# An mLSTM cell and a gated product on one core: gates of four chunks in one call, and half passes for the second chunk's first product

## The chip, the cores and the metric

One Trainium2 chip, one of its cores. The kernel is one program with its instructions in the order in which the source issues them, one stream for each engine: PE (TensorE), DVE (VectorE), ACT (ScalarE), POOL (GpSimd) and SP (SyncE, which here only issues DMAs). ACT and POOL issue some DMAs too. The metric is the device time of one execution in microseconds (us). The time of a kernel is the median over its runs.

## The reference, cut to what matters

Eight inputs and one output, all float32. B = 4 batches, H = 8 heads, S = 768 steps, head dimension D = 40; the second part takes 3072 rows (b, s) of 320 values.

```
for t in range(S):                                  # for each b, h
    m_new  = max(f[t] + m, i[t])
    C = exp(f[t] + m - m_new) * C + exp(i[t] - m_new) * outer(v[t], k[t])
    n = exp(f[t] + m - m_new) * n + exp(i[t] - m_new) * k[t]
    m = m_new
    y[t] = sigmoid(o[t]) * (C @ q[t]) / max(|n . q[t]|, 1)
x = y as (B*S, H*D) = (3072, 320)
h = x @ w_in                                        # 320 -> 2048
out = (h * sigmoid(1.702 * h)) @ w_out              # 2048 -> 320
```

The maximum m runs through time; within a chunk of steps it is a running sum of f and a running maximum (a scan), and from one chunk to the next only one value for each (b, h) is carried.

## The kernel before, in words

**Chunks.** Time is cut into six chunks w = 0 to 5 of L = 128 steps. A chunk has three stages: attention (the recurrence as a masked product within the chunk, plus a carried state), the first product, called "up" (512 rows of x by w_in), and the second product, "down" (by w_out). The attention of chunk w+1 is laid between the blocks of the down stage of chunk w (function `attention` gives the order, `run(side.get(i, []))` at line 1342 issues it after block i). Chunk 0 has an up of its own in full float32 (`up`), and its down (`down`) has 16 blocks. Later chunks' downs (`down_fast`, from line 1023) have 14 blocks.

**The order of the work** is written by hand (`manual_schedule`): each engine runs its instructions in source order, and an instruction that waits holds up all that is behind it on its engine or queue. Data dependences become semaphore waits. Buffers come from pools that turn round by tag; a tile waits until the last user of its buffer has finished.

**Gates.** `gates(w)` (line 302) works on 32 partitions, one for each (b, h), with 128 steps beside each other: two scans, the maximum at the half and at the end of the chunk, the differences that the weights need, and a swap of the two halves of 64 steps for the odd heads (by the factors `odd` and `even`, which `masks()` makes). `gates_out(w)` (343) stores the results to DRAM in five DMAs (`m_row`, `st_row`, `d_row`), `columns_in(w)` (371) loads them back with time on the partitions (`raw`, five DMAs) and `spread(w)` (423) loads `m_row`, broadcast to 64 partitions, into the two `wt` tiles (four DMAs, L430). `columns_turn`, `columns` and `weights_exp` (466) turn these into the weights. `side_queue(w)` sends the DMAs of chunk 1 by POOL's queue and the others by SP's. The call for chunk 1 stands at j = 3 of chunk 0's up, that of chunk 2 at j = 0 of chunk 1's up, those of chunks 3 to 5 at block 7 of the down two chunks before. `load_gates(w)` issues two loads for each chunk.

**The up stage of chunk 1 and later.** A float32 product is built of several passes of type fp32r: x and w_in are each split into a part rounded by the factor BIAS (`x_high`, `w_high`) and the rest in two forms (`x_low`, `x_diff`, `w_low`, `w_diff`); results come from two sums in PSUM, `side` and `main`. The 16 blocks of 128 columns go in eight pairs j = 0 to 7. The 320 features of x are two groups of 128 and a last one of 64. For chunk 1, `up_fast` (848) does 16 passes of 128x128 by 512 for each pair, 128 in all, the last 64 features in full passes too (`x_rest`, `w_rest`). For chunks 2 to 5, `up_strips` (923) does the last 64 features in passes that use 64 of the 128 rows of the array, and it does the terms `low`, `high`, `diff` as such half passes for every pair from the second on: `halves` issues two that lie on different halves of the rows and run at the same time. They need one more weight, `w_strip` (for chunk 2 on made by `strip_weights`, 777, in chunk 1's down), and one more split of x (the last lines of `split_on`, line 835).

**Notes.** Of two sets of half passes that add to the same bank, the second may start only when the first has finished. `seen` (917) puts an empty instruction on ACT's queue which waits for the first set; the first pass of the second set waits for that note (`behind`, 912).

```
    def seen(w, mm):
        note = (A if w + 1 < NW else nc.sync).nop()
        tc.add_manual_dep(note.ins, mm.ins.name, SYNC)
```

**Around each pair:** `evict_side` (963, ACT) scales `side` into g; `evict_main` (968, DVE, L971) adds `main`; `gelu_fast` (840, ACT) applies the gelu in place; POOL makes differences and sums for the down stage.

**The splits of w_in** are made once, in four quarters n of 256 rows by 512 columns: `split_high` (740, ACT), `split_diff` (743, DVE L745), `split_low` (748, DVE L751). Quarters 0 and 1 before chunk 1's up, 2 and 3 within it. `keep` (753) stores `w_diff` of each quarter and `w_low` of quarters 2 and 3 to DRAM from ACT's queue (L755), and later chunks fetch them. `keep_last` (757) copies `w_low` of quarter 3 into another tile on ACT, and SP stores that at j = 5.

**Counting.** `count` adds up to `COUNTS[w]` semaphore increments to PE's stream, one behind a pass; nothing waits for them.

The loop over j of chunks 1 to 4 (lines 1231 to 1296) issues `up_fast` or `up_strips`, then whatever of the splits, stores, fills and transposes for the next chunk belongs to that j:

```
for j in range(NF // 2):
    (up_strips if by_strips(w) else up_fast)(w, j)
    ...
        if j == 2:
            split_high(3)
            keep(w_diff_row, 2, w_diff[1, 2])
            keep(w_low_row, 2, w_low[1, 2])
            split_diff(3)
            split_low(3, V)
```

Of the kernel before, what the change touches and what calls it, by code (L numbers as in the profile page):

```python
# [8 lines left out]
FP = mybir.dt.float32  # L9
# [16 lines left out]
COUNTS = {0: 54, 1: 128, 2: 105, 3: 105}  # L26
# [9 lines left out]
def kernel(  # L36
# [178 lines left out]
    one1 = const.tile([BH, 1], FP, name="one1")  # L215
# [3 lines left out]
    ones = one1.to_broadcast([BH, L])  # L219
# [9 lines left out]
    odd, even = (const.tile([3 * BH, 1], FP, name=n) for n in ("odd", "even"))  # L229
# [10 lines left out]
    cols, stacked, m_row, raw = {}, {}, {}, {}  # L240
# [61 lines left out]
    def gates(w):  # L302
# [30 lines left out]
        if w:  # L333
            for x in range(2):
                V.tensor_scalar(out=swapped[:, x * HL:(x + 1) * HL], in0=st[:, (1 - x) * HL:(2 - x) * HL], scalar1=odd,
                                scalar2=None, op0=OP.mult)
            V.scalar_tensor_tensor(out=swapped, in0=st, scalar=even, in1=swapped, op0=OP.mult, op1=OP.add)
            both = ends[w] = gate.tile([BH, 2], FP, name="both")
            V.tensor_tensor(out=both[:, 0:1], in0=m, in1=mid, op=OP.subtract)
            V.tensor_tensor(out=both[:, 1:2], in0=mid, in1=end, op=OP.subtract)  # L340
            stacked[w] = m_run, swapped, both

    def gates_out(w):
        m_run, swapped, both = stacked[w]
        to = m_row[w] = rows.tile([2, BH, HL], FP, name="m_row")
        side_queue(w).dma_start(out=to[:, 0::2].rearrange("n h t -> h n t"),
                          in_=m_run[0::2].rearrange("h (n t) -> h n t", t=HL))
        for n in range(2):
            side_queue(w).dma_start(out=to[1 - n, 1::2], in_=m_run[1::2, n * HL:(n + 1) * HL])
        st_row = rows.tile([L // 32, 3 * BH, 32], FP, name="st_row")  # L350
        d_row = rows.tile([BH, 2], FP, name="d_row")
        stacked[w] = st_row, d_row
        side_queue(w).dma_start(out=st_row.rearrange("n k t -> k n t"), in_=swapped.rearrange("k (n t) -> k n t", t=32))
        side_queue(w).dma_start(out=d_row, in_=both)
# [11 lines left out]
    def masks():  # L366
        V.tensor_reduce(out=odd, in_=full.rearrange("p (j two) -> p two j", two=2)[:, 1], axis=AX.X, op=OP.add)
        V.memset(odd[BH:2 * BH, :], 0.0)
        V.tensor_scalar(out=even, in0=odd, scalar1=-1.0, scalar2=1.0, op0=OP.mult, op1=OP.add)

    def columns_in(w):
# [3 lines left out]
        for n in range(L // 32):  # L375
            side_queue(w).dma_start(out=x[n * 32:n * 32 + 32, 0:3 * BH].rearrange("r (k t) -> r k t", t=32),
                              in_=st_row[n].rearrange("(k r) t -> r k t", r=BH))
# [46 lines left out]
    def spread(w):  # L424

        for c in range(2):
# [281 lines left out]
    w_high, w_low, w_diff, w_rest = {}, {}, {}, []  # L708
# [11 lines left out]
    def by_strips(w):  # L720
        return w > 1

    def rooms(w):
# [4 lines left out]
        if w > 1:  # L728
            w_low.update({(w, n): gp.tile([128, 2, 512], FR, tag="g", name="w_low")
                          for n in ((2, 3) if by_strips(w) else (2,))})  # L730
# [4 lines left out]
    def more_rooms(w):  # L735

        w_low[w, 3], w_diff[w, 2], w_low[w, 2], w_diff[w, 3] = (gp.tile([128, 2, 512], FR, tag="g", name=name)
                                                                for name in ("w_low", "w_diff", "w_low", "w_diff"))
# [18 lines left out]
    def keep_last():  # L757
        w_low[3] = work.tile([128, 2, 512], FR, tag="wx", bufs=1, name="w_low")
        A.copy(out=w_low[3], in_=w_low.pop((1, 3)))

# [15 lines left out]

    def strip_weights():

        wr = w_rest[0]
        w_rest.append(work.tile([128, NF // 2, 128], FR, tag="wx", bufs=1, name="w_strip"))  # L780
        d, low, high = w_rest[1], wr[64:128], wr[0:64]
# [12 lines left out]
    def split_x(w, c):  # L794
# [9 lines left out]
        A.activation(out=x_rest[w][0][:, t], in_=x[:, 2], func=AF.Copy, scale=BIAS if by_strips(w) else -BIAS / BASE)  # L804
# [9 lines left out]
    def split_x_rest(w, c):  # L814
        t, x = part_of(w, c)
        both, other = x_rest[w]
        if by_strips(w):
            V.scalar_tensor_tensor(out=other[:, t], in0=both[:, t], scalar=-1.0 - 1.0 / BASE, in1=x[:, 2], op0=OP.mult,
                                   op1=OP.add)
        else:  # L820
            V.scalar_tensor_tensor(out=other[:, t], in0=x[:, 2], scalar=-1.0 / BASE, in1=both[:, t], op0=OP.mult,
                                   op1=OP.subtract)
# [6 lines left out]
    def split_on(w):  # L829
# [5 lines left out]
        if by_strips(w):  # L835
            both, other = x_rest[w]
            V.scalar_tensor_tensor(out=both[64:128], in0=other[64:128], scalar=BASE, in1=both[64:128], op0=OP.mult,
                                   op1=OP.add)
# [8 lines left out]

    def up_fast(w, j):

        n = j // 2  # L850
        col = lambda i: slice((2 * j + i) % 4 * 128, (2 * j + i) % 4 * 128 + 128)
        low = w_low.get((w, n), w_low.get(n))
        if j % 2:
            side, main = ([bank() for _ in range(2)] for _ in range(2))
        else:
            side, main = ([both[:, i, :] for i in range(2)] for both in (banks("p_h"), banks("p_h")))
        parts = [(main, k, lambda i, k=k: w_high[n][:, k, col(i)], x_high[w][:, k]) for k in range(2)]
        parts += [(main, 2 + k, lambda i, k=k: low[:, k, col(i)], x_low[w][:, k]) for k in range(2)]
        parts += [(side, k, lambda i: w_rest[0][:, 2 * j + i], x) for k, x in enumerate(x_rest[w])]
        parts += [(side, 2 + k, lambda i, k=k: w_diff[w, n][:, k, col(i)], x_diff[w][k]) for k in range(2)]  # L860

        def passes(which, i, first=False, last=False):
            for m in which:
# [555 lines left out]
```

## Time and profile before

| | us |
|---|---|
| median of three runs | 438.42 |
| the runs | 437.18, 438.42, 440.49 |
| the profiled execution: its time | 438.98 |
| its span in the trace | 437.3 |

The stages in the trace, each from its first pass to that of the next (microseconds from the start of the span):

| from | to | length | what runs on PE |
|---|---|---|---|
| 0.00 | 108.15 | 108.15 | all stages of chunk 0, attention of chunk 1 |
| 108.15 | 137.79 | 29.64 | up of chunk 1 |
| 137.79 | 176.63 | 38.84 | down of chunk 1, attention of chunk 2 |
| 176.63 | 204.71 | 28.08 | up of chunk 2 |
| 204.71 | 243.47 | 38.76 | down of chunk 2, attention of chunk 3 |
| 243.47 | 271.72 | 28.25 | up of chunk 3 |
| 271.72 | 437.30 | 165.58 | the rest |

How to read the lines below. A line of the windows gives start, end and length of a stretch, then busy time and number of instructions of PE, PEld (weight loads), DVE, ACT and POOL, then the granted TensorE clock (1.00 is full speed), the busy share of the DMA engines and GB/s. A line of the timeline gives start and duration, engine, source line, operation, the tiles out<-in with their shapes, and in brackets how long the engine stood idle before it and what ended that. "q" behind an engine's name is its queue of instructions that are not counted as busy, such as DMA issues. A line of DMA issues gives the number of issues, KB each and the median us from issue to landing.

### The profile page before, as it was taken

The numbers are of one execution on the slowest core, as the hardware profiler recorded it, in microseconds if no ns is written. First come the engines' busy times: TensorE is split into PE (matmuls) and PEld (weight loads), VectorE is DVE, ScalarE is ACT, GpSimd is POOL, SyncE is SP. The second block draws the span as 40 slices with busy tenths as digits, with TensorE's granted clock in tenths as the row PEclk, the third lists the DMA queues.
The fourth block names the chain that finished last, engine by engine and source line by source line (L and its number), as shares of the span: only waits on it lengthen the run. The fifth ranks groups of instructions, "written<-read, shape, count | busy, mean of one in ns | idle before, by whom it ended". The sixth has DMA issues, their size and how long they took to land.

```text
span 437.3 us, 13451 instructions
## 1 busy us (share of the span) xinstructions
PE 431.9 (99%) x5342; PEld 375.0 (86%) x5342; DVE 353.5 (81%) x689; ACT 247.2 (57%) x540; POOL 146.7 (34%) x155
## 2 busy tenths in 40 slices
PE   8999999999999999999999999999999999999996
PEld 6877887777888999888999888999887999888996
DVE  4898998989889799659789659789759759779990
ACT  5677779922777900397900386900287940298720
POOL 6411326533056822035712035622036624013100
PEclk9999999999999999999999999999999999999999
DMA  8999999217797516999306997605998925820000
GB/s 169 188 285 193 254 252 225 66 34 186 198 206 152 127 49 156 312 161 172 54 31 146 311 178 154 86 19 131 282 197 151 121 66 125 258 98 2 0 32 30
DMA packets 130733, 64.07 MB, mean 147 GB/s; under 512 B 102208, under 2 KB 122672, under 8 KB 130672
## 3 DMA queue, kind: packets, MB, share of 16 engines
q1 hardware_dynamic: 121232, 57.48, 59.4%
q10 hardware_dynamic: 8768, 4.28, 3.4%
q0 software_dynamic: 672, 1.46, 1.2%
q8 instruction: 43, 0.70, 0.7%
q14 instruction: 18, 0.15, 0.1%
HBM read 51.86 MB, written 11.34 MB: 145 GB/s over the span
## 4 chain that ended last, share of the span: by engine, by line
PE 94%; ACT 2%; DVE 1%; DMA 1%; issue 0%; SPq 0%; DVEq 0%
PE p_out L1036 26%; PE p_h L911 13%; PE p L911 10%; PE p_out L979 8%; PE p_h L663 7%; PE p L1114 5%; PE p L865 3%; PE p_h L865 3%; PE p L931 3%; PE p L540 2%; PE p L548 2%; PE p L496 2%; PE p_h L673 2%; PE p_out L1114 2%; PE p L639 2%; PE p L412 1%
## 5 line engine op out<-in xcount | busy, mean ns | idle before, releaser
L803 ACT ACTIVATE x_high<-xT 128x512 fp32r<-128x512 f32 x10 | 6.3, 631 | 88.4 <-DVE xT L609 88.4
L1036 PE MATMUL p_out<-w_out,g 128*128 128x160 f32 x384 | 55.5, 301 | 0.0
L1036 PEld LDWEIGHTS p_out<-w_out,g 128*128 128x128 f32 x384 | 52.9, 190 | 1.6 <-ACT g L966 1.3
L843 ACT ACTIVATE g<-g 128x512 f32<-128x512 f32 x80 | 45.7, 629 | 1.9 <-DVE g L971 1.6
L1004 POOL TENSOR_TENSOR g<-g 128x512 f32<-128x512 f32 x16 | 20.5, 1302 | 69.9 <-ACT g L843 63.1
L971 DVE SCALAR_TENSOR_TENSOR g<-p,g 128x512 f32<-128x512 f32 x40 | 25.7, 684 | 22.5 <-PE p L911 19.2
L966 ACT ACTIVATE g<-p 128x512 f32<-128x512 f32 x40 | 21.7, 596 | 34.9 <-PE p L911 29.8
L469 ACT ACTIVATE wt<-wt,cols 128x64 f32<-128x64 f32 x160 | 38.9, 335 | 0.1
L1036 PE MATMUL p_out<-t_sb,s 128*128 128x160 f32 x256 | 37.8, 301 | 0.0
L1036 PEld LDWEIGHTS p_out<-t_sb,s 128*128 128x128 f32 x256 | 35.5, 190 | 0.2
L979 PE MATMUL p_out<-w_out,g 128*128 128x320 f32 x128 | 35.7, 436 | 0.0
L971 DVE SCALAR_TENSOR_TENSOR g<-p_h,g 128x512 f32<-128x512 f32 x40 | 25.7, 687 | 11.9 <-PE p_h L911 11.9
L979 PEld LDWEIGHTS p_out<-w_out,g 128*128 128x128 f32 x128 | 24.0, 190 | 9.5
L1021 POOL TENSOR_TENSOR s<-g,s 128x256 f32<-128x256 f32 x16 | 12.9, 835 | 52.8 <-PE p_out L1036 52.8
L663 PE MATMUL p_h<-xT,w_in 128*128 128x256 f32 x128 | 29.8, 385 | 0.1
L663 PEld LDWEIGHTS p_h<-xT,w_in 128*128 128x128 f32 x128 | 23.6, 190 | 5.4 <-issue 2.2
L966 ACT ACTIVATE g<-p_h 128x512 f32<-128x512 f32 x40 | 21.6, 593 | 10.3 <-PE p_h L911 9.2
L476 POOL TENSOR_SCALAR_AFFINE_SELECT wt<-wt 64x1024 f32<-64x1024 f32 x20 | 24.3, 1214 | 6.9 <-ACT wt L469 6.0
L625 POOL TENSOR_TENSOR vw<-v_st,cols 128x656 f32<-128x656 f32 (+1 forms) x13 | 16.7, 1301 | 25.0 <-PE p_out L1036 15.4
L1041 DVE TENSOR_TENSOR o_sb<-o_sb,p_out 128x160 f32<-128x160 f32 x56 | 16.3, 314 | 9.7 <-PE p_out L1036 9.2
L421 DVE STREAM_TRANSPOSE qT<-q_sq 128x512 f32<-128x512 f32 x20 | 20.4, 1109 | 1.2 <-ACT q_sq L122 1.2
L911 PE MATMUL p_h<-x_diff,w_diff 64*128 64x512 f32 x128 | 20.3, 395 | 0.0
(260 smaller groups left out, 1097.2 us busy)
## 6 DMA issues: line engine op xcount, KB each, us to landing
w_diff<-w_row SPq DMA_DIRECT2D x16, 512.0 KB, 4.8
wt<-m_row SPq DMA_DIRECT2D x20, 256.0 KB, 5.3
bits<-in_moe_w_in_dram SPq DMA_DIRECT2D x8, 512.0 KB, 9.5
w_low<-w_row SPq DMA_DIRECT2D x8, 512.0 KB, 6.2
out_dram<-o_sb SPq DMA_DIRECT2D x24, 160.0 KB, 2.9
q_sq<-in_q_dram SPq DMA_DIRECT2D x10, 320.0 KB, 8.1
eo<-in_o_gate_dram SPq DMA_DIRECT2D x5, 640.0 KB, 7.4
bits<-in_moe_w_out_dram SPq DMA_DIRECT2D x8, 320.0 KB, 5.4
```

The lines of the kernel that those rows point to most:

```text
L469: A.activation(out=x[:, h, :], in_=x[:, h, :], func=AF.Exp, scale=-1.0, bias=cols[w][:, c * PH + h:c * PH + h + 1])
L476: G.affine_select(out=r, in_=r, compare_op=OP.is_ge, fill=0.0, base=0, pattern=[[0, PH], [1, HL]], channel_multiplier=-1)
L663: T.matmul(ph[j][i][:, t], w_in[f // 4][:, c, f % 4 * 128:f % 4 * 128 + 128], x[:, c, t], start=(first and c == 0 and n == 0), stop=(not f ...
L843: A.activation(out=g, in_=g, func=AF.Gelu_apprx_sigmoid)
L865: T.matmul(dst[i], a(i), x, start=(first and m == which[0]), stop=(last and m == which[-1]))
L911: mm = T.matmul(to[f], a(f)[r], x[r], start=(first and n == 0), stop=(last and n + 1 == len(parts)))
L966: A.activation(out=g[:, i, :], in_=opened[w, j][0][i], func=AF.Copy, scale=-BASE)
L971: V.scalar_tensor_tensor(out=g[:, i, :], in0=opened[w, j][1][i], scalar=1.0 + 1.0 / BASE, in1=g[:, i, :], op0=OP.mult, op1=OP.add)
L979: T.matmul(po, gs[w, f // 2][:, f % 2, b * L:(b + 1) * L], w_out_sb[f // NH][:, f % NH, :], start=(f == 0), stop=(f == NF - 1))
L1004: G.tensor_tensor(out=a10, in0=a00, in1=a10, op=OP.subtract)
L1036: T.matmul(po, a(f), b[:, f, :], start=(f == 0), stop=(f == NH - 1))
L1114: T.matmul((main, side, main)[n], g_part[n, b, f // 2][:, f % 2], wo[n, f][0][:, wo[n, f][1]], start=(f == order[0] and n < 2), stop=(f == ...
```

## The change

It has these parts.

1. **Chunk 1's up by half passes.** `up_fast` is gone and `up_strips` serves chunk 1 too. The weight it needs, `w_strip[1]`, is made by a new `first_strip` (one DVE operation of 128x1024, at block 9 of chunk 0's down, from `rest_high` and `rest_low`). `split_x` and `split_x_rest` lose their second form, and the extra DVE split at the end of `split_on` is done for chunk 1 as well. Chunk 1's increments start at pair 0 instead of pair 1 and number 154; `down_fast` has a `count(1)` behind each pass for those that are left over.
2. **The order in chunk 1's up.** The splits of quarter 3 move from j = 2 to j = 3 (`split_high(3)` stays at j = 2 but behind a fill), both of its stores go out by ACT's queue at j = 3, and `keep_last` with SP's store goes; so `w_low` of quarter 3 stays in its first tile, now of pool `sp`. The fill of `q_sq` moves from j = 3 to j = 2, the transposes that follow it from j = 3 to j = 2, and the second half of the broadcast of `m_row` from j = 2 to j = 7. Gelus come in the order of a table `late`.
3. **Gates of chunks 1 to 4 at once.** `load_four` loads the gates of four chunks into 128 partitions (eight loads on SP's queue, ahead of chunk 1's k), `gates_four` runs once in place of `gates(1)`, and `four_out` stores the results of some chunks: chunk 1's on POOL's queue in the old place, those of chunks 2 to 4 together by SP at block 3 of chunk 0's down. `gates` stays for chunks 0 and 5.
4. **Masks:** `odd` and `even` have 128 rows; ahead of `gates(5)` 32 of them are set back by two memsets.

```diff
-COUNTS = {0: 54, 1: 128, 2: 105, 3: 105}
+COUNTS = {0: 54, 1: 154, 2: 105, 3: 105}
...
+    def load_four():
+        x = work.tile([L, 768], FP, tag="y", name="gates4")
+        four["in"] = [x[:, n * L:(n + 1) * L] for n in range(4)]
+        for n, src in enumerate((f_gate, i_gate)):
+            for x in range(4):
+                nc.sync.dma_start(out=four["in"][n][x * BH:(x + 1) * BH],
+                                  in_=src[:, :, (x + 1) * L:(x + 2) * L].rearrange("b h s -> (b h) s"))
+
+    def gates_four():
...
+        V.tensor_tensor_scan(out=f_run, data0=ones4, data1=f, initial=0.0, op0=OP.mult, op1=OP.add)
+        V.tensor_tensor(out=a, in0=i, in1=f_run, op=OP.subtract)
+        V.tensor_tensor_scan(out=m_run, data0=ones4, data1=a, initial=NEG, op0=OP.mult, op1=OP.max)
+        V.tensor_copy(out=m[0:BH], in_=m_at[1])
+        for n in range(4):
+            r = slice(n * BH, (n + 1) * BH)
+            V.scalar_tensor_tensor(out=m[(n + 1) * BH:(n + 2) * BH] if n < 3 else m_at[NW - 1], in0=m_run[r, L - 1:L],
+                                   scalar=m[r], in1=f_run[r, L - 1:L], op0=OP.max, op1=OP.add)
+        V.tensor_scalar(out=m_run, in0=m_run, scalar1=m, scalar2=None, op0=OP.max)
...
+    def four_out(queue, w0, w1):
+        m_run, swapped, both = (x[(w0 - 1) * BH:(w1 - 1) * BH] for x in four["out"])
...
+        store_max(queue, to, m_run)
+        queue.dma_start(out=st_row.rearrange("k n h t -> h (k n) t"),
+                        in_=swapped.rearrange("h k (n t) -> h (k n) t", t=32))
+        queue.dma_start(out=d_row, in_=both)
...
-    def spread(w):
+    def spread(w, cs=range(2)):
...
-        w_low[w, 3], w_diff[w, 2], w_low[w, 2], w_diff[w, 3] = (gp.tile([128, 2, 512], FR, tag="g", name=name)
-                                                                for name in ("w_low", "w_diff", "w_low", "w_diff"))
+        w_low[w, 3] = sp.tile([128, 2, 512], FR, tag="g", name="w_low")
+        w_diff[w, 2], w_low[w, 2], w_diff[w, 3] = (gp.tile([128, 2, 512], FR, tag="g", name=name)
+                                                   for name in ("w_diff", "w_low", "w_diff"))
...
-    def keep_last():
-        w_low[3] = work.tile([128, 2, 512], FR, tag="wx", bufs=1, name="w_low")
-        A.copy(out=w_low[3], in_=w_low.pop((1, 3)))
...
+    def first_strip():
+        w_strip[1] = work.tile([128, NF // 2, 128], FR, tag="wt", bufs=2, name="w_strip")
+        V.scalar_tensor_tensor(out=w_strip[1], in0=rest_high, scalar=-1.0 / BASE, in1=rest_low, op0=OP.mult, op1=OP.add)
...
-    def up_fast(w, j):
...
-        late = j < 3 and w + 1 < NW
-        for n in ((), (), (0, 1))[j] if late else (j - 1,) if w + 1 < NW or j + 1 < NF // 2 else ():
+        late = {1: (), 2: (), 3: (0, 1), 4: (2,), 5: (3, 4)} if w == 1 else {1: (), 2: (0, 1)} if w + 1 < NW else {7: ()}
+        for n in late.get(j, (j - 1,)):
             gelu_fast(w, n)
...
-    load_gates(1)
-    load(1, "k")
...
     seam(0, 0, 1)
+    load_four()
+    load(1, "k")
...
                 if j == 3:
                     masks()
-                    gates(1)
-                    gates_out(1)
+                    gates_four()
+                    four_out(G, 1, 2)
                     columns_in(1)
...
-                (up_strips if by_strips(w) else up_fast)(w, j)
+                up_strips(w, j)
...
                     if j == 2:
-                        split_high(3)
                         keep(w_diff_row, 2, w_diff[1, 2])
                         keep(w_low_row, 2, w_low[1, 2])
+                    if j == 3:
                         split_diff(3)
                         split_low(3, V)
-                        sums_from = w_low[1, 3].bitcast(FP)[:, 0, :]
-                    if j == 3:
                         keep(w_diff_row, 3, w_diff[1, 3])
-                        keep_last()
-                        wait_for(sums_from)
+                        wait_for(w_low[1, 3].bitcast(FP)[:, 0, :])
                         weight_sums(2)
-                    if j == 5:
-                        keep(w_low_row, 3, w_low[3], nc.sync)
-                if more and j in (1, 3):
-                    fill_squares(q_sq if j == 3 else k_sq)
+                        keep(w_low_row, 3, w_low[1, 3])
+                if more and j in (1, 2 if w == 1 else 3):
+                    fill_squares(k_sq if j == 1 else q_sq)
+                if w == 1 and j == 2:
+                    split_high(3)
...
-                    spread(w + 1)
+                    spread(w + 1, range(1 if w == 1 else 2))
                     load(w + 1, "k")
-                if more and j:
-                    for n in ((), (), (0, 2), (4, 6), (1, 3), (5, 7), ())[j - 1]:
+                if w == 1 and j == 7:
+                    spread(2, (1,))
+                if more:
+                    for n in {2 if w == 1 else 3: (0, 2), 4: (4, 6), 5: (1, 3), 6: (5, 7)}.get(j, ()):
                         block_transposes(w + 1, n)
...
+            if w == 0 and i == 3:
+                four_out(nc.sync, 2, NW - 1)
...
                 split_diff(0)
                 split_low(0, V)
+                first_strip()
```

## The prediction

> **What bounds the kernel now.** I read the page's busy times first, then the chain of work that ended last, then the stages one by one. Times of day are microseconds from the start of the span.
>
> ```profile
> PE 431.9 (99%) x5342; PEld 375.0 (86%) x5342; DVE 353.5 (81%) x689; ACT 247.2 (57%) x540; POOL 146.7 (34%) x155
> PEclk9999999999999999999999999999999999999999
> PE 94%; ACT 2%; DVE 1%; DMA 1%; issue 0%; SPq 0%; DVEq 0%
> ```
>
> TensorE is in flight for 431.9 of 437.3 and 94% of the chain is its own passes. So a microsecond is won only by a pass that goes away, and lost only where PE must wait. The granted clock is at its top digit in all slices.
>
> The stretches between the first pass of an "up" stage and the first `p_out` pass after it, for chunk 1 (to be changed) and chunk 2 (already by half passes), with busy times in the order PE, PEld, DVE, ACT, POOL:
>
> ```profile
> 108.15:137.79 29.64, 29.64 (x130) 24.22 (x129) 26.30 (x43) 22.47 (x39) 12.49 (x10) 1.00 0.78 191
> 176.63:204.71 28.08, 28.08 (x231) 22.40 (x230) 19.30 (x29) 18.36 (x33) 10.05 (x8) 1.00 0.99 210
> ```
>
> Both stages are PE without a gap. Chunk 1 has 128 full passes; chunk 2 does the product in 120 pass times and is 1.56 shorter. But DVE is busy for 26.3 of 29.6 in chunk 1 and for 19.3 of 28.1 in chunk 2: chunk 1 also splits the weights. The timeline gives the places that matter, two engines of chunk 1 and then chunk 2:
>
> ```profile
> 112.90 1.29 DVE L971 SCALAR_TENSOR_TENSOR g<-p,g 128x512 f32<-128x512 f32 x2 [1.24 <-ACT g L966]
> 117.44 1.27 DVE L971 SCALAR_TENSOR_TENSOR g<-p_h,g 128x512 f32<-128x512 f32 x2
> 118.64 1.20 DVE L745 SCALAR_TENSOR_TENSOR w_diff<-w_high,w_in 128x1024 fp32r<-128x1024 f32 x1
> 119.77 1.21 DVE L751 TENSOR_TENSOR w_low<-w_in,w_high 128x1024 fp32r<-128x1024 f32 x1
> ...
> 114.23 0.84 ACTq L755 DMA_DIRECT2D w_row<-w_diff  x2
> 121.46 0.45 ACTq L755 DMA_DIRECT2D w_row<-w_low  x1
> ...
> 176.63 1.20 PE L931 MATMUL p<-x_high,w_high 128*128 128x512 f32 x4
> 191.44 0.63 PE L911 MATMUL p<-x_low,w_low 64*128 64x512 f32 x4
> 193.73 0.63 PE L911 MATMUL p<-x_low,w_low 64*128 64x512 f32 x4
> ...
> 191.71 1.29 DVE L971 SCALAR_TENSOR_TENSOR g<-p_h,g 128x512 f32<-128x512 f32 x2 [2.16 <-PE p_h L911]
> ```
>
> To be seen: the store at 114.23 needs only `w_diff` tiles finished by 111, yet starts 0.04 after the eviction of 112.90 to 114.19, for which the gelu ahead of it on ACT's queue waits. ACT's queue stands still at an unmet wait and everything behind it stands too. And in chunk 2 the fourth pair's main eviction starts 15.08 after the first pass, and the fifth pair's second set of half passes 17.10 after it.
>
> **The change part by part.** *Half passes for chunk 1.* Removed: 128 passes; added: 120 pass times (12 full, 216 half passes that run in twos). Chunk 2 gives 28.08 for this, chunk 3 28.25 by its own first passes (243.47 to 271.72), so the gain is 1.56 or 1.39. I take 1.56.
>
> *The wait that comes with it.* Each second set of half passes waits for a note: an empty ACT instruction that itself waits for the first set (line 919). The old form had no notes. A note stands in ACT's queue behind whatever the program put there before it. The change puts the stores of the last weight quarter (its `w_diff` and `w_low`, from DVE's lines 745 and 751) behind pair 3 and so ahead of pair 4's note. With chunk 1's first pass at 108.15, pair 3's main eviction can start at 108.15 + 15.08 = 123.23. DVE gets there in time: pair 1's eviction at 116.34 (by 184.82 - 176.63), two splits until 119.89, pair 2's eviction until 121.0, two transposes of 2.02 until 123.0. Then by the spacing of the rows above: 1.20 for the eviction, 1.13 for the first split, 1.22 for the second: `w_low` is ready at 126.78. ACT then issues the store, 0.45, and passes the note at 127.2. PE wants to begin its second set at 108.15 + 17.10 = 125.25. Stall: about 1.95 if the issue holds the note back, 1.53 if not; no less than that unless the eviction comes before its product. The upper end, if pair 2's work is a microsecond late, is 3. I take 1.9. Behind the note stand pair 4's side eviction and three gelus, which then run late by as much; they feed evictions and the second product, both after 138.
>
> The trace has no PE gap of this length to show what it does to the clock: from 5 to 430 it shows granted 1.00 and no wait longer than some tenths. [...]
>
> *The end of the stage.* PE leaves it at 137.79 - 1.56 + 1.9 = 138.1. DVE's last transposes then end at 138.6 and the last eviction starts there (138.74 before); ACT's gelus, table load and exponentials (142.73 before) keep their places. The old stall of 0.22 at 151.4, where `p_s` waits for DVE's L648, stays. Nothing is added.
>
> *Splits before the stage.* DVE gets `first_strip` (as L745: 1.22) and one more 64x512 split (as chunk 2's L837: 0.69). They push the second half of `x_high` (ready 106.80) by some 0.8 to 107.6 against the first pass at 108.15, and `x_rest` to 110.8 against its pass 3.8 after the first, 112.0. Cost 0, hidden by the last passes of the first down stage; with that cover gone, 1.9. Off the path: ACT's copy of 1.05 (line 759) goes, a fill and a high split move in ACT's queue ahead of pair 3's note: they wait for the store of 119.9, and the note goes by about 121 against 121.8.
>
> *Gates.* Three calls go (114.11 to 117.44; 165.78 to 170.85; one like it in chunk 3), with their stores and later loads. PE runs through all of them without a gap: 0. The call for four chunks replaces the first (47.07 to 50.51): the same operations with 128 partitions, longer by a copy, three more row steps (0.15 to 0.25 each) and twice the width in the swaps: 1.3. The next things DVE makes for PE end at 52.96 and are read at 55.94, and DVE waits 0.42, 0.66 and 1.22 for ACT at 62.2, 69.7 and 75.4, so this is absorbed. Cost 0, at most 0.6 were the cover gone.
>
> *Loads.* SP issues eight gate loads where two stood, ahead of chunk 1's k:
>
> ```profile
> 28.23 0.33 SPq L102 DMA_DIRECT2D fi<-in_f_gate_dram  x1
> 29.50 0.32 SPq L102 DMA_DIRECT2D fi<-in_i_gate_dram  x1
> 31.60 7.83 SPq L134 DMA_DIRECT2D t_sb<-in_k_dram  x3
> 56.37 3.50 SPq L430 DMA_DIRECT2D wt<-m_row  x4
> ```
>
> A load waits for the one eight before it, so they go at the pace at which weight loads land, to about 39; k follows (4 to 5 of issue) to 43.5 instead of 39.4, and SP stays 4 late. k lands by 52 (row: 9.3) and is read at 55.06. The broadcast of `m_row` lands at 66 for the first half (8.5 after issue), now at up to 70; ACT's exponentials begin at 70.11. Cost 0, by a small margin. The five stores for chunks 2 to 4 go in SP's free time between 69 and 94.
>
> Sum: the profiled execution took 438.98 (span 437.3 and 1.68 around it). 438.98 - 1.56 + 1.9 = 439.3. It lies 0.56 above the median of the runs, 438.42; the median to expect is **438.8**.
>
> **The rivals.** *No stall.* ACT passes pair 4's note in time, because DVE reaches the last splits earlier or ACT's queue lets the note by. For it: PE, ACT and DVE work are each less than the stage. Against it: the start at 114.23, and a DVE that can't evict before PE has finished. Time: 438.42 - 1.56 = 436.9.
>
> *The same wait, longer.* The last two stores also share counters with transfers of `raw` (the built program lists these waits), issued behind chunk 2's v:
>
> ```profile
> v_st<-in_v_dram SPq DMA_DIRECT2D x2, 160.0 KB, 10.8
> raw<-st_row SPq DMA_DIRECT2D x4, 12.0 KB, 3.8
> ```
>
> The `raw` transfers need the first stores to land (114.5 + 5.9, by the row of `w_diff` stores) and go out by 122.5; at 3.8 they land at 126.3, just under 126.78. From 126.8 on this decides. At 10.8 it is 133: a stall of 8, of which half is likelier. Time: 438.8 + 2 to 6 = 441 to 445. Against it: the like transfers of chunk 3 landed in 2.7.
>
> *A late broadcast before chunk 1.* If the first half of `wt` lands after 70.11, ACT's exponentials, its fill of `q_sq` (74.07), DVE's transposes (75.36) and its evictions up to 82.92 move as much, and the second scores of PE at 83.55 wait for the last of these. It decides from 70.7, where 0.6 of slack is used up. With k and weights all 7 late, 73: 2.4. Time: 439.5 to 441.3, slower. For it: SP is never idle from 28 to 55. Against it: the transfers are bound by bytes there, and these stay.
>
> That the half passes are not done is no rival: the built program lists them.
>
> **How the numbers follow.** Stall eats the gain: 0.50, own range 437.8 to 439.9. No stall: 0.20. Longer wait: 0.15. Late broadcast: 0.12. Rest: 0.03. No stall at its low end is 436.3 (runs spread by 0.5 here and more); the longer wait is taken to 442.0, which leaves its far end out. A measurement of this kernel can't tell less than about 1% (4.4) from no change. Faster by more needs three times the gain in sight: 0.03. Slower by more (above 442.8) is the far part of the longer wait and a little of the broadcast: 0.09. Within: 0.88.
>
> **What would show it.** Right: PE idle once, 1.5 to 2 long, near 125 to 127, ended by ACT's queue right after the store of `w_low`; the stage from first pass to first `p_out` about 30.0. First step wrong: passes further apart than 0.23. Second wrong: no gap and a stage of 28.1. Loads wrong: a gap at 83. Gates wrong: any gap before 65. The forecast fails most if a `raw` transfer lands after 127.

## The result and the profile after

The changed kernel takes 444.22 us (median of six runs, 442.10 to 445.73) against 438.28 for the kernel before in the same rounds; the ratio is 1.0125, 95% interval 1.0085 to 1.0164. It is slower by 1.25%, and above the range that was forecast. Medians below are over all runs; the ratios leave disturbed runs out and lie near the ratio of the means, so that the two can differ by some tenths of a per cent, and where they do, the ratio is used. The profiled execution took 445.73, span 444.0: 6.75 above the profiled execution of before.

The page's busy times and granted clock of the kernel after:

```profile
PE 434.0 (98%) x5442; PEld 373.8 (84%) x5442; DVE 344.8 (78%) x658; ACT 247.4 (56%) x539; POOL 146.7 (33%) x155
...
PEclk9999999899999999999999999999999999999999
...
PE p L1130 5%; PE p_h L923 3%; PE p L923 3%; PE p_out L1130 2%; DMA q_sq<-x_rest 1%; DMA x_rest<-y 1%; PE p L945 1%; ACTq L650 0%; SPq L659 0%; DVE o_sb L1139 0%; DVE xT L666 0%; DVE o_sb L1057 0%; DVE x_diff L866 0%; DVE o_sb L1055 0%; DVEq L1139 0%
```

PE's busy share hardly falls, 99% to 98%, while the kernel is 6.7 longer: a pass at the slower clock is in flight longer and counts as busy (below, 16 passes take 5.81 in place of 4.58). One digit of the clock is an 8. The chain, last line, is new too: in before it was PE's passes back to the start; here, followed back from the end, it leaves PE at chunk 5 and goes through the loads and stores of x_rest, where it breaks off. The stretches say more; the kernel after, from first down of chunk 0 to the up of chunk 1, a piece of it, the up of chunk 1, and the up of chunk 5 (columns as before: start, end, length, busy times, granted clock, DMA share, GB/s):

```profile
65.90:111.52 45.62, 44.62 (x642) 32.38 (x641) 38.73 (x65) 28.39 (x65) 20.74 (x18) 0.96 0.64 136
85.76:89.17 3.41, 3.41 (x29) 2.51 (x29) 3.38 (x5) 3.40 (x4) 0.00 (x0) 0.50 0.64 147
111.52:141.79 30.27, 28.42 (x231) 22.32 (x229) 25.72 (x33) 21.03 (x38) 11.29 (x9) 1.00 0.92 231
381.53:433.14 51.61, 50.19 (x374) 43.28 (x374) 45.20 (x93) 32.60 (x72) 7.92 (x8) 1.00 0.17 62
```

and the first and the last of these stages in the kernel before (its up of chunk 1 stands in the prediction):

```profile
65.68:108.15 42.47, 42.47 (x643) 31.14 (x641) 38.24 (x64) 26.98 (x62) 20.13 (x18) 1.00 0.55 125
377.16:426.56 49.40, 49.40 (x376) 43.66 (x375) 42.11 (x85) 32.19 (x71) 7.95 (x8) 1.00 0.18 56
```

So 6.7 of span are 3.15 in the first down (45.62 - 42.47), 0.63 in chunk 1's up (30.27 - 29.64), 2.21 in chunk 5's up (51.61 - 49.40), 0.56 in chunk 2's up (28.64 against 28.08) and 0.2 elsewhere. Only the second of these was in the forecast. The 0.56 is not followed here; in the other kernels with half passes this stage took 28.22 to 28.26. PE's waits in the kernel after, the three that are new (total, times, longest):

```profile
PE p L923 <- ACTq L931: 1.8, 1, 1.8
PE p L945 <- DVE x_diff L866: 1.3, 1, 1.3
PE p L553 <- DVE state L705: 0.9, 2, 0.6
```

**First place, near 83.** The timeline of the kernel after, SP, then ACT, then PE, and last the scores of the kernel before:

```profile
28.41 5.56 SPq L348 DMA_DIRECT2D gates<-in_f_gate_dram  x4
35.59 4.22 SPq L348 DMA_DIRECT2D gates<-in_i_gate_dram  x4
61.22 3.13 SPq L487 DMA_DIRECT2D wt<-m_row  x4
...
65.59 0.69 ACT L257 ACTIVATE w_out<-bits 128x512 f32<-128x512 f32 x1 [1.46 <-DMA bits<-in_moe_w_out_dram]
...
83.35 1.16 PE L553 MATMUL p<-qT,kT 40*64 40x64 f32 x64 [0.59 <-DVE state L705]
84.82 1.88 PE L553 MATMUL p<-qT,kT 40*64 40x64 f32 x64 [0.31 <-DVE state L705]
86.63 5.81 PE L994 MATMUL p_out<-w_out,g 128*128 128x320 f32 x16
...
82.47 2.10 PE L496 MATMUL p<-qT,kT 40*64 40x64 f32 x128
```

SP is 4.85 late at the broadcast (61.22 against 56.37). But what ACT waits for is neither k nor the broadcast: it is a piece of w_out, which the same queue loads between the two. ACT's exponentials start at 71.94 instead of 70.11, DVE's additions of the carry end as much later, and the scores wait 0.59 and 0.31. Then the clock is granted at 0.50 for 3.41, and the next 16 passes, 4.58 before, take 5.81.

**Second place, chunk 1's up:** the forecast stall, at 130.76. DVE and then ACT's queue and PE:

```profile
126.73 1.29 DVE L986 SCALAR_TENSOR_TENSOR g<-p_h,g 128x512 f32<-128x512 f32 x2 [0.19 <-PE p_h L923]
127.94 1.22 DVE L800 SCALAR_TENSOR_TENSOR w_diff<-w_high,w_in 128x1024 fp32r<-128x1024 f32 x1
129.07 1.22 DVE L806 TENSOR_TENSOR w_low<-w_in,w_high 128x1024 fp32r<-128x1024 f32 x1
...
130.32 0.33 ACTq L810 DMA_DIRECT2D w_row<-w_low  x1
...
130.76 0.73 PE L923 MATMUL p<-x_low,w_low 64*128 64x512 f32 x4 [1.85 <-ACTq L931]
```

Eviction, two splits, the store, the note, PE: the chain of the prediction, 1.85 where it had 1.9.

**Third place, the start of chunk 5's up,** four chunks away from anything edited. ACT's queue stores x, SP loads it back, DVE turns it, PE reads it; the last two lines are the same store and load in the kernel before:

```profile
371.09 1.43 ACTq L650 DMA_DIRECT2D x_rest<-y  x2
375.98 0.36 SPq L659 DMA_DIRECT2D q_sq<-x_row  x1
376.45 1.23 SPq L659 DMA_DIRECT2D q_sq<-x_rest  x2
382.68 0.63 DVE L666 STREAM_TRANSPOSE xT<-q_sq 128x128 f32<-128x128 f32 x2 [2.67 <-DMA q_sq<-x_rest]
384.07 0.73 PE L945 MATMUL p<-x_diff,w_diff 128*128 128x512 f32 x2 [1.34 <-DVE x_diff L866]
...
367.51 1.30 ACTq L593 DMA_DIRECT2D x_rest<-y  x2
369.92 0.37 SPq L602 DMA_DIRECT2D q_sq<-x_row  x1
```

In the kernel before, this load came 2.4 after the start of the x_rest stores (369.92 against 367.51); here it comes 4.9 after (375.98 against 371.09). Of the 2.21 by which the stage is longer the wait is 1.34; PE's busy time is 0.79 longer too, which is not explained here. What the DMA engines did from 373.0 to 375.5 (busy share in tenths, GB/s, queues):

```profile
DMA  9999999999878875431000011000101000000000
GB/s 514 279 248 209 178 217 230 220 238 203 180 148 156 129 115 84 74 53 23 12 14 12 0 25 8 8 12 4 12 8 12 16 12 16 12 16 20 14 12 14
...
q8 instruction: 1, 0.02, 3.6%
```

The stores are done at 374 but for a trickle at 8 to 20 GB/s, and in this window one packet of 16 KB on a queue named "instruction" (43 packets and 0.70 MB in the whole kernel before, 44 here). It starts at 373.0 and takes 1.44. The kernel before has such a packet too, but at 365.9, ahead of its x_rest stores. Such a packet is called a fetch below; that it brings PE's instructions is inferred from the runs in which it moves with their number.

### The profile page after: what moved, and what is told of

Read it like the earlier page. It is cut to its first block, busy times and chain, and to the rows that moved or that the text cites. A ratio compares the mean times of both kernels' runs of the same rounds, so it can differ in the third digit from the quotient of the medians.

```text
span 444.0 us, 13654 instructions
## 1 busy us (share of the span) xinstructions
PE 434.0 (98%) x5442; PEld 373.8 (84%) x5442; DVE 344.8 (78%) x658; ACT 247.4 (56%) x539; POOL 146.7 (33%) x155
## 5 line engine op out<-in xcount | busy, mean ns | idle before, releaser
L994 PE MATMUL p_out<-w_out,g 128*128 128x320 f32 x128 | 36.9, 447 | 0.0
L923 PE MATMUL p_h<-x_diff,w_diff 64*128 64x512 f32 x160 | 25.4, 395 | 0.0
L923 PE MATMUL p_h<-x_low,w_low 64*128 64x512 f32 x160 | 25.0, 390 | 0.0
L923 PE MATMUL p_h<-x_high,w_high 64*128 64x512 f32 x160 | 24.9, 390 | 0.0
```

The lines of the kernel that those rows point to most:

```text
L923: mm = T.matmul(to[f], a(f)[r], x[r], start=(first and n == 0), stop=(last and n + 1 == len(parts)))
L994: T.matmul(po, gs[w, f // 2][:, f % 2, b * L:(b + 1) * L], w_out_sb[f // NH][:, f % NH, :], start=(f == 0), stop=(f == NF - 1))
```

## The experiments

Theory after the result: three separate losses, late weight loads (first down), the note behind the stores (chunk 1's up), and the one in chunk 5. The rival: half passes as such are what costs. The kernel before, timed beside each, gave 438.5 to 438.6.

| kernel | median | ratio to before (95%) |
|---|---|---|
| repeat | 445.66 | 1.0136 (1.0105 to 1.0167) |
| gates_apart | 446.97 | 1.0185 (1.0150 to 1.0220) |
| stores_later | 442.06 | 1.0071 (1.0042 to 1.0099) |
| gates_apart_later | 442.57 | 1.0095 (1.0064 to 1.0125) |
| before_102 | 441.17 | 1.0078 (1.0046 to 1.0109) |
| phase_180 | 441.86 | 1.0080 (1.0047 to 1.0113) |
| two_loads | 440.83 | 1.0073 (1.0044 to 1.0102) |
| all_three | 437.59 | 0.9987 (0.9967 to 1.0008) |
| gates_alone | 439.36 | 1.0046 (1.0020 to 1.0071) |
| gates_alone_two | 438.62 | 1.0006 (0.9984 to 1.0028) |
| apart_later_180 | 440.52 | 1.0051 (1.0032 to 1.0070) |
| sums_after | 438.43 | 1.0000 (0.9985 to 1.0015) |

**repeat**: the changed kernel once more.

> The changed kernel once more, as the mark for the others. Theory (late weight loads): the gap ahead of chunk 1's scores near 83 is there in every profile, 0.5 to 1.2 long, because ACT waits near 65 for a w_out piece; whether the granted clock falls to 0.5 for 3.4 behind it differs from run to run, as some runs of the changed kernel show a mean clock of 0.996 and some 1.000. Time 442 to 445.5. The stall of pair 4 near 129 is there at 1.8 to 2.0. The gap of 1.34 at the start of chunk 5's up (x_rest loaded late) is taken to be chance: it should be gone or of another size. Rival (the loss in chunk 5 belongs to the change): it is there again at 1 to 2.

All three waits again: 2.9 near 83 (2.6 the longer), 1.85 at 130.97, 1.48 at 384.04. The last was not chance: there the rival holds.

**gates_apart**: the change without parts 3 and 4.

```diff
+    load_gates(1)
+    load(1, "k")
...
-    load_four()
-    load(1, "k")
...
-                    gates_four()
-                    four_out(G, 1, 2)
+                    gates(1)
+                    gates_out(1)
...
+                    if w == 1:
+                        gates(2)
```

> The change without its gates of four chunks: half passes and the new order in chunk 1's up, the gates, masks and loads as before. Theory (late weight loads): SP is no longer 4 late, ACT doesn't wait for the w_out piece near 65, no gap near 83, clock 1.00; the stall of pair 4 stays at 1.8 to 2.0, so the stage of chunk 1's up is 29.9 to 30.3 and the time 438.3 to 439.3, that is 0 to 1 above before and 4 to 6 below the repeat. Rival (the half passes and their order cost it all, the gap at 83 is given back later): 441 or more.

The gap near 83 is gone (first down 42.47) and yet the kernel is the slowest of all. PE's waits, and ACT behind its stores:

```profile
PE p L866 <- ACTq L874: 4.8, 1, 4.8
PE p L866 <- DVE g L929: 1.6, 1, 1.6
```

```profile
130.81 0.60 ACTq L753 DMA_DIRECT2D w_row<-w_low  x1
131.54 1.09 ACT L924 ACTIVATE g<-p 128x512 f32<-128x512 f32 x2 [3.55 <-DMA raw<-st_row]
```

The old call for chunk 2 puts 3.3 of DVE work into chunk 1's up (28.69 busy), an eviction comes 1.6 late; and its results pass through DRAM into `raw` at that time, so that the stores of the last quarter, which share counters with the `raw` loads, are held until 130.8: the "same wait, longer" of the prediction, in the kernel that lacks the part which prevents it. Behind the wait of 4.8 the granted clock falls, to 0.95 on average over chunk 1's up, which takes 36.59. The forecast of 438.3 to 439.3 fails. My reading that the removed gate calls were worth nothing held only beside full passes.

**stores_later**: the two stores of quarter 3 behind pair 4.

```diff
-                        keep(w_diff_row, 3, w_diff[1, 3])
                         wait_for(w_low[1, 3].bitcast(FP)[:, 0, :])
                         weight_sums(2)
+                    if j == 4:
+                        keep(w_diff_row, 3, w_diff[1, 3])
                         keep(w_low_row, 3, w_low[1, 3])
```

> The changed kernel with the two stores of the last weight quarter behind pair 4 in place of pair 3. Theory (the note of pair 4 stands behind the stores): the stall near 129 goes, nothing follows in its place, stage 28.1 to 28.5, time 1.7 to 2.1 below the repeat. Rival (the note stands behind DVE's late eviction or ACT's table load anyway): the stall stays at 1 or more and the time within 0.7 of the repeat.

No stall; chunk 1's up and the down behind it:

```profile
107.80:136.20 28.40, 28.40 (x231) 22.32 (x229) 25.30 (x33) 20.62 (x37) 9.42 (x8) 1.00 1.05 241
136.20:175.88 39.68, 38.93 (x738) 37.83 (x737) 33.89 (x65) 17.24 (x48) 19.66 (x16) 1.00 0.39 88
```

The stage is 1.87 shorter than with the stall, as expected, but the down takes 39.68 where it took 38.64: chunk 2's scores wait 0.74 for DVE's additions. So "nothing follows in its place" fails, and the two stages together gain 0.83. By ratio the gain is 0.65% of the time, 2.9, each ratio with an interval of about 1.3 to either side; what the traces don't account for is left open.

**gates_apart_later**: both edits.

> Both of these at once: half passes with the old gates and the stores of the last quarter behind pair 4. Theory (the two losses are separate and add): no gap near 83 and none near 127, stage 28.1 to 28.5, 1.2 to 1.6 below before: 436.7 to 437.1. Rival (they are one loss, or a third stands behind): no lower than before.

The theory of two separate losses fails: 1.0095. DVE's late eviction stays (1.45), a wait for a note of 1.02 too, PE stands for 1.05 near 150, for which the profile names nothing, and chunk 5's up waits 1.89. A third loss was open, the one in chunk 5: every kernel so far with half passes in chunk 1 has it.

**before_102**: the kernel before with 26 empty increments fewer on PE, and nothing else.

```diff
-COUNTS = {0: 54, 1: 128, 2: 105, 3: 105}
+COUNTS = {0: 54, 1: 102, 2: 105, 3: 105}
```

> The kernel before with 102 empty increments in chunk 1's up in place of 128, and nothing else. [...] Theory (fetch in the way): PE now waits 0.5 to 1.9 at the start of chunk 5's up for x_diff, the stage to the last down is 50.8 to 52 instead of 49.4, time 1.3 to 2.4 above before. Rival (the wait in chunk 5 comes from the changed loads, stores or DMA order): time within 0.4 of before, no wait.

As the theory has it: 2.6 above before by the medians, 3.4 by the ratio. Its chunk 5's up and PE's new wait:

```profile
376.53:428.10 51.57, 50.40 (x375) 43.99 (x374) 45.27 (x93) 32.62 (x72) 8.02 (x8) 1.00 0.18 62
```

```profile
PE p L931 <- DVE x_diff L811: 1.1, 1, 1.1
```

and its half microseconds around the fetch, which starts at about 368.7 and takes 0.88 (the last two columns are the DMA share and GB/s):

```profile
368.50:369.00 0.50, 0.50 (x6) 0.50 (x5) 0.50 (x2) 0.00 (x0) 0.50 (x1) 1.00 0.61 115
369.00:369.50 0.50, 0.50 (x6) 0.50 (x5) 0.50 (x4) 0.00 (x0) 0.50 (x1) 1.00 0.00 0
369.50:370.00 0.50, 0.50 (x6) 0.50 (x5) 0.50 (x3) 0.00 (x0) 0.50 (x2) 1.00 0.08 8
370.00:370.50 0.50, 0.50 (x6) 0.50 (x5) 0.50 (x2) 0.00 (x0) 0.50 (x2) 1.00 0.08 14
```

After the fetch the rest of the stores of x trickles at a share of 0.08, little more than one engine of sixteen. That the fetch sits on just that engine is my inference; the packets don't name their engine. The late load of x (371.21) then falls behind the load of w_out by POOL (640 KB, 370.99), which in the kernel before came after it (371.61 against 369.92). So 26 instructions that do nothing decide 0.8% of the time. That just 26 would do it was not read from a trace; this run shows that they do. The place of the fetch can be read in all 14 profiles of this document. It starts either 11.1 to 11.3 ahead of the first pass of chunk 5's up (365.9 against 377.16 in the kernel before) or 7.9 to 8.9 ahead (368.7 against 376.53 here, 373.0 against 381.53 in the kernel after), when the x_rest stores are on their way. In the seven profiles with the later place PE waits 0.54 to 1.89 for x_diff and the stage takes 50.77 to 52.13; in the seven with the earlier one there is no such wait and the stage takes 49.20 to 49.43, except in phase_180 below. So in before the fetch costs nothing that shows (49.40), and in before_102 about 2.6 by the medians.

**phase_180**: the changed kernel with 180 increments, 26 more: 256 more PE instructions than before in place of 230.

```diff
-COUNTS = {0: 54, 1: 154, 2: 105, 3: 105}
+COUNTS = {0: 54, 1: 180, 2: 105, 3: 105}
```

> The changed kernel with 180 empty increments in place of 154, and nothing else: PE's instruction fetches from chunk 2 on fall where they fell before. Theory (fetch in the way): no wait at the start of chunk 5's up, that stage 49.3 to 49.7, 1.3 to 2.4 below the repeat (445.66): 443.3 to 444.4; the gap near 83 and the stall near 129 stay. Rival (loads or DMA order): as the repeat, 445 to 446, the wait of 0.5 to 1.9 stays.

2.5 below the repeat by the ratios, a little more than the theory has. But the profiled run still shows a wait of 0.59 there and that stage at 50.84 in place of 49.3 to 49.7, though its fetch is at before's place (368.8, 11.1 ahead of the stage): the load of x_rest starts 3.6 after its stores. Why is open, so the theory holds for the time and not for this profile. The same trace has the stall of 1.85 in chunk 1's up followed by 3.41 of half clock (stage 31.83), which the repeat and the first profile, with the same stall, do not have.

**two_loads**: stores_later with the gates loaded by two DMAs.

```diff
-            for x in range(4):
-                nc.sync.dma_start(out=four["in"][n][x * BH:(x + 1) * BH],
-                                  in_=src[:, :, (x + 1) * L:(x + 2) * L].rearrange("b h s -> (b h) s"))
+            nc.sync.dma_start(out=four["in"][n],
+                              in_=src[:, :, L:5 * L].rearrange("b h (x s) -> x (b h) s", s=L))
```

> The changed kernel with the gates of four chunks loaded by two DMAs in place of eight, and the stores of the last quarter behind pair 4. The same bytes in a quarter of the issues. Theory (eight issues ahead of chunk 1's k hold SP up, since each waits for the load eight before it): SP reaches m_row's broadcast by about 57.5 instead of 60 to 62, ACT waits for w_out pieces less than 0.5 in all between 50 and 70, no gap near 83; 1.0 to 2.5 below the kernel with the later stores alone (442.06). Rival (the loads are bound by bytes and landing, not by issues): ACT still waits 1.4 or more near 57 to 65, time within 0.5 of 442.06.

```profile
26.75 0.66 SPq L347 DMA_DIRECT2D gates<-in_f_gate_dram  x1
27.96 0.56 SPq L347 DMA_DIRECT2D gates<-in_i_gate_dram  x1
56.30 2.61 SPq L486 DMA_DIRECT2D wt<-m_row  x4
```

SP is on time, ACT waits for no piece, no gap near 83. The time can't be told from stores_later's (1.0073 against 1.0071), and the gain of 1.0 to 2.5 fails: the mechanism is shown, the gain is not, here. In the profile chunk 5's up took 51.57, 0.80 more than in stores_later's, which may hide part of it.

**all_three**: two loads, stores behind pair 4, 180 increments.

> The changed kernel with all three mended: two loads, the stores behind pair 4, 180 increments. If the three losses are separate: 442.06 less 1.0 to 2.5 for the loads less 1.3 to 2.2 for chunk 5, so 437.4 to 439.7, about the time of before (438.6). What keeps it from 437 is that chunk 2's scores wait 0.7 for DVE near 150, as with the later stores alone, where the next stage took 39.7 in place of 38.7. Rival (one loss hides another): 440.5 or more.

```profile
109.00:137.33 28.33, 28.33 (x230) 22.32 (x228) 25.30 (x33) 20.63 (x37) 9.41 (x7) 1.00 1.02 242
137.33:176.80 39.47, 38.94 (x739) 37.83 (x737) 34.31 (x66) 17.25 (x48) 19.46 (x16) 1.00 0.39 94
377.64:426.84 49.20, 49.20 (x375) 43.59 (x374) 42.04 (x85) 32.20 (x71) 7.88 (x8) 1.00 0.16 54
```

The three add: no gap in chunk 5 (49.20), none in chunk 1's up, 0.9987: the kernel before, within the interval.

**gates_alone** and **gates_alone_two**: the kernel before with parts 3 and 4 alone, by eight loads and by two.

> The kernel before with the gates of four chunks alone (eight loads, one call, masks): no half passes in chunk 1's up, old order, PE's stream and so its fetches as before. Theory (eight loads hold SP and the w_out pieces up): ACT waits 1.4 to 5 in all for w_out pieces between 50 and 67, PE stands 0 to 2.6 ahead of chunk 1's scores, first down 42.7 to 48 long (42.5 before), sometimes with 3.4 at half clock; median 439.5 to 442. Chunk 1's up stays 29.6. Rival (the late pieces cost only together with the half passes): within 0.5 of before.

> The same with two gate loads in place of eight. Theory (the number of issues): no wait for w_out pieces above 0.5, no gap above 0.3 ahead of chunk 1's scores, within 0.8 of before: 437.8 to 439.4. The three calls of gates on DVE that go bring nothing by themselves, since PE ran through them. Rival (the one call with 128 partitions is late itself): raw and the exponentials 1 or more late, time as gates_alone.

By eight loads 1.0046, by two 1.0006: the issues cost 1.8 by the ratios, with an interval of some 1.5 to either side, and 0.7 by the medians (439.36, just under the range expected); this is so without half passes too. The profile with eight shows the large form, a wait of 2.6 and the half clock (0.96 on average from 63.65 to 111.97; 16 passes behind the wait take 6.26 in place of 4.58):

```profile
PE p L553 <- DVE state L705: 2.9, 2, 2.6
```

Nine of its runs lie at 438.7 to 440.7, three at 442.9 to 443.7, and these three have a mean clock of 0.996, so most of the 1.8 comes from the runs with the half clock.

**apart_later_180**: all_three but with the old gates and their loads.

> Half passes with the old gates, the stores behind pair 4 and 180 increments: against all_three (437.59) only the gates differ. Theory (DVE is full in chunk 1's up, and the old call for chunk 2 on it, 3.3, makes its evictions late): PE waits 1.4 near 117 for an eviction and about 1 near 131, that stage 30.8 to 31.3 instead of 28.3; no wait at chunk 5; 440 to 441. Rival (the old gates cost nothing beside half passes, as PE ran through them before): 437 to 438.

As the theory has it: chunk 1's up 31.44, DVE 28.61 busy in it, waits of 1.48 and 1.32; 1.0051 against 0.9987. The gates of four, loaded by two DMAs, are worth nothing alone and 2.8 beside half passes.

**sums_after**: all_three with two differences of DVE (2.04) behind the carry's additions.

```diff
-                lambda: (product(total(2), t2, (o01, o11)), last_sums(w, c, range(4) if c else (0, 1), G if c else V)),
+                lambda: (product(total(2), t2, (o01, o11)), (c or w > 1) and last_sums(w, c, range(4) if c else (0, 1), G if c else V)),
...
+            if w == 1 and i == 3:
+                last_sums(1, 0, (0, 1))
```

> all_three with DVE's first two differences for chunk 1's down (L1035, 2.04) behind the carry's additions of chunk 2 instead of ahead of them. Theory (chunk 2's scores wait for these additions because DVE comes late out of the shorter up stage): the two gaps of 0.22 and 0.31 near 150 go, the down stage of chunk 1 takes 38.6 to 38.9 instead of 39.5, 0.5 to 0.8 below all_three: 436.8 to 437.1. Rival (DVE is as late with what follows, the score products' eviction or the sum's own reader): the gap only moves, within 0.3 of 437.6.

The gap only moves, as the rival has it: DVE is in time now, but PE stands at the same scores and the profile names nothing that it waits for ("issue"). The down takes 39.86, and 438.43 is above both forecasts. That DVE's lateness makes this stage long is therefore not shown.

```profile
150.70 0.69 PE L552 MATMUL p<-qT,kT 40*64 40x64 f32 x29 [0.25 <-issue]
```

## Why the prediction was wrong, point by point

- *Half passes for chunk 1*, 1.56 gained: right in kind. Without the stall the stage took 28.40 and 28.33, a gain of 1.24 to 1.31. A term it lacked: the down behind it takes back 0.6 to 1.0 of that (39.47 to 39.86 against 38.84, in the four kernels without the stall). Waits for DVE are part of it (0.74 in stores_later); what keeps the stage long in sums_after, where they are gone, is open.
- *The wait that comes with it*, 1.9: right in place, cause and size (1.85). The stage was to be about 30.0 and was 30.27. The rival "no stall" was what stores_later had to build.
- *The clock*: the sum has no term for it, and the trace of before had no gap of this length to tell. In chunk 1's up nothing was lost to it in the two profiles of the changed kernel (1.00 over the 30.27 of the kernel after), but in phase_180 the same stall is followed by 3.41 at 0.50. The 3.41 ahead of the fall and the 3.41 at the slower clock in phase_180, then the 3.41 ahead of the fall near 83 in the kernel after:

```profile
123.87:127.28 3.41, 1.56 (x16) 0.96 (x14) 2.59 (x3) 3.26 (x6) 0.69 (x2) 1.00 0.76 152
127.28:130.69 3.41, 3.41 (x20) 2.66 (x18) 1.42 (x3) 1.79 (x4) 3.41 (x2) 0.50 1.05 308
...
82.35:85.76 3.41, 2.41 (x107) 1.74 (x106) 3.27 (x8) 3.41 (x5) 2.19 (x3) 1.00 0.53 92
```

  In phase_180 PE is busy for 1.56 of the stretch ahead of the fall, with the whole stall in it; ahead of 85.76 it is busy for 2.41, mostly with small passes of 40x64, and idle for 1.00. The kernel after has a stall of the same 1.85 in chunk 1's up and keeps its clock there, so the length of the stall does not decide alone. What does is not shown.
- *Loads*, "cost 0, by a small margin": the step that failed near 83. SP's 4 late were right (4.85), k and the broadcast were followed and came in time; the pieces of w_out that stand on the same queue between them (L181, two groups of 7 and 10 issues) were not. They cost 1.8 by the ratio of gates_alone to gates_alone_two, and the stage is 3.15 longer in the profile of the kernel after, half clock included. The rival "late broadcast" had place and direction but not the transfer, and no clock.
- *Gates*, "PE runs through all of them without a gap: 0": right for the old up (gates_alone_two 1.0006), wrong for the new one, which has no room on DVE for the old call.
- *What was not in the sum*: the 230 instructions that the change adds to PE's stream. I counted them as passes and wrote of the increments that nothing waits for them. The sum put them at nothing without a reason: this is the other step that failed. Such instructions move later fetches: the one ahead of chunk 5's up starts 11.2 ahead of the stage in before, 7.9 with 26 instructions fewer (before_102), 8.5 with 230 more (the kernel after) and 11.1 with 256 more (phase_180). By the ratios of the pairs before_102 to before, phase_180 to repeat and all_three to two_loads this is worth 2.5 to 3.8, each with an interval of 1.4 to 2 to either side; in the profiles of these pairs chunk 5's up differs by 0.9 to 2.4. By the ratios it is the largest term of the loss; in the profile of the kernel after the first down is larger (3.15 against 2.21).
- *The sum*: +0.3 forecast; the parts as the runs size them are about -1.3 and +1.9 for the half passes and their wait, +1.8 for the loads (half clock behind their gap included), +2.5 to 3.8 for the fetches, and at times 1.6 for a half clock behind the stall (31.83 against 30.27): 4.9 to 6.2 without the last, near the 5.5 to 6 measured. The intervals of the parts are too wide for more than that. The chance of 0.09 for slower by over 1% was too small, because all rivals lay near the edit.

## What to carry to other kernels

When a load is put ahead on a queue, list every transfer behind it up to the first slack, not only those that the change names: the one that bound was two groups further on. In a kernel at 99% of one engine, count the instructions that an edit adds to that engine's stream: here 26 of them moved a fetch by 3.3 us against a tight store and load four chunks away, at 2.6 us by the medians, and a few empty instructions can be tried as a knob before an edit is judged. And a saving on the bound engine is kept only where the second engine has room in the same stage; here the half passes with the old gates came out at 1.0051 and with the gates of four at 0.9987, which is still not told from the kernel before.

## What the runs showed of the hardware

- Packets of 16 KB go over a queue named "instruction", among the data: 43 in the kernel before, 44 in the kernel after; those at 373.0 in the kernel after and at 368.7 in before_102 took 1.44 and 0.88 us. That they bring PE's instructions is inferred from their places in four runs whose PE streams differ in length (11.2, 7.9, 8.5 and 11.1 us ahead of chunk 5's up in before, before_102, the kernel after and phase_180). Where one met the last of a store of small rows, the load behind that store started 4.9 us (the kernel after) and 5.1 us (before_102) after the store's start, in place of 2.4 in before. That both sit on one DMA engine is inferred.
- The granted clock fell to 0.50 for 3.41 us in the kernel after (85.76 to 89.17) and in phase_180 (127.28 to 130.69). PE had been busy for 2.41 of the 3.41 ahead of the first fall, mostly with passes of 40x64, and for 1.56 ahead of the second, with passes of 64 rows. It fell in gates_alone too, behind a wait of 2.6 (0.96 on average from 63.65 to 111.97), and in gates_apart in the stage with a wait of 4.8 (0.95 over 36.59). In the kernel after it stayed at 1.00 through a stall of 1.85. What decides is not shown.
- Eight gate loads of 16 KB each in place of two of 64 KB, for the same bytes, put SP's queue 4.9 us behind at the broadcast (61.22 in the kernel after against 56.30 in two_loads). In the kernel after they wait 9.5 in all for weight loads ahead of them to land, each once, 2.3 at most.
